# First layer, first sweep and the change to the second: the same operations issued at other slots

## The chip, the core and the metric

The kernel runs on one core of one Trainium2 chip. The metric is the device time of one execution in microseconds (us); each kernel is run several times and the median is compared. The core has TensorE (PE, with the load of its weights shown as PEld), VectorE (DVE), ScalarE (ACT), GpSimd (POOL) and SyncE (SP). Each engine takes its instructions in the order in which they are written for it, and waits at one until the semaphores it needs are there. POOL and SP do nothing here but start DMA transfers.

## The reference

Three steps follow one another. All arrays are fp32.

```
# attention: 8 batches x 8 heads, 576 positions in chunks of 64, head size 64
scores = (q_c @ k_c.T) / 8;  attn = softmax(scores);  out = attn @ v_c
x = out as (4608 tokens, 512)
# layer 1: w_gate, w_val 512 x 1536, w_out 1536 x 512
g = x @ w_gate;  x = (g * sigmoid(g) * (x @ w_val)) @ w_out
# layer 2: w_in 512 x 2048, w_out 2048 x 512
h = x @ w_in;  y = (h - tanh(h)) @ w_out
```

## The kernel before

**Numbers.** An fp32 operand is held as two fp32r tiles: a high half (a cast, step h...) and a low half (a subtraction of the high half from the operand, step l...). A product takes three passes (high by high, high by low, low by high). The high half is made by DVE or ACT, as the table ON says; the low half by DVE (`halves`, L436).

**Tiling.** The 4608 tokens are 9 batches of 512. A unit is one batch by one pair of 128 hidden columns. Sweep 0 does pairs 0 to 2 of layer 1 for all batches, sweep 1 pairs 3 to 5 (and adds the partial result x2p of sweep 0), sweep 2 the 8 pairs of layer 2. A name such as vs0_4_2_1 says sweep 0, batch 4, third unit, second column block. Each in-projection of a unit is made of seven products at 128x256 in place of eight (`product`, `in_proj`, L653 and L667). They run in the order B11, B21, T2, T1, T3, B22, T4, where T1 to T4 are sums of quarters of x and of w, into two PSUM banks X and Y (Xg, Yg for the gate, Xv, Yv for the values). Partial results are copied out on the way by ACT ("snaps": s<-Xv, s<-Yv), and DVE adds them to the bank later. The product that follows in the same bank waits for that copy or addition. A unit issues 14 products and 8 pieces of out-projection (acc), whose hidden tiles h are those of the unit two before it.

**Preparing x.** While a unit runs, x of the next batch is split for the seven products (`x_set`, L741): four sums (s0 to s3, subtractions on DVE), seven high halves (hB11 ...) and seven low halves (lB11 ...), in tiles xb14_B11 and so on. In sweep 0 x comes from attention. It is computed for four tiles of 128 rows a batch, during the units of the batch before: transposes of q and k on DVE (tq, tk: qT, kT, L873), scores on PE (sc, L887), maximum and difference on DVE for two halves (c0, c1: mx and scratch, L796 and L299), the exponential on ACT (e, L801), sum and reciprocal on DVE (n: sm, L805 to L807), the division on DVE (m, L302), a transposition on PE (ppt, L823), its copy by ACT, and the output on PE (po, L898), which ACT copies to xra (x of the next batch). Scores, ppt and po share the two PSUM banks a0 and a1.

**Order.** The tables at the head of the file set the order. AT gives each step a slot relative to the START of its set, ON the engine. One PE piece (a product, or a piece of out-projection, by the letters of PE) is written per slot, and then the steps that are due (`tick`, L311):

```
while later and later[0][0] < now[0] + 1:
    heapq.heappop(later)[-1]()
now[0] += 1
```

So a slot sets no time. It sets where a step stands in the queue of its engine, relative to the other steps of that engine. Between engines only semaphores order the work. Sets that matter here: a (attention tile), x0 (split of x in sweep 0), x1 (in sweep 1), g0 and g1 (silu, product and halves of h in sweep 0 and 1), ge (the same for the last units of sweep 0), fc1 and fr1 (weights for sweep 1: columns of w_gate and w_val, rows of w_out, read back from a scratch copy in HBM: f_wv, f_wo), ah (the preparation of that copy: magnitude on ACT, four bit operations on DVE; cvt_wv, raw_wv).

Of the kernel before, what the change touches and what calls it, by code (L numbers as in the profile page):

```python
# [29 lines left out]
    "ah.ld": -6.5, "ah.mag": 9.5, "ah.cl": 11.5, "ah.sh": 11.5, "ah.sg": 12.5, "ah.tl": 13,  # L30
# [12 lines left out]
    "g1.l0": 19.5, "g1.h1": 22, "g1.l1": 23, "a.lq": -19.5, "a.lv": 4, "a.tq": -8.5, "a.tk": -4,  # L43
    "a.s": 0, "a.c0": 1.5, "a.c1": 2.5, "a.e": 3, "a.n": 7, "a.m": 9, "a.p": 12.5, "a.o": 14.5,
    "ge.silu0": 14.5, "ge.silu1": 12.5, "ge.m1": 21, "ge.m0": 20.5, "ge.h0": 23, "ge.l0": 24.5,
    "ge.h1": 24, "ge.l1": 32, "dr.ld": -19.5, "dr.mag": 9, "dr.cl": 11, "dr.sh": 11.5,
    "dr.sg": 13, "dr.tl": 13, "dr.h": 16.5, "dr.l": 17.5, "dc.ld0": -14, "dc.mag0": 0,
# [1430 lines left out]
```

## Time and profile before

| | |
|---|---|
| median of 3 runs | 1757.7 us (1754.9 to 1758.71) |
| profiled execution | 1756.21 us, its span 1754.4 us |
| mean granted TensorE clock | 0.994 |
| PE busy | 1712.4 us, 98% of the span |
| DVE busy | 1381.9 us, 79% |
| ACT busy | 1135.8 us, 65% |
| POOL busy | 136.5 us, 8% |
| chain that ended last | PE 83%, DVE 8%, SP's queue 4%, DMA 3% |

The span runs from the first to the last instruction; the profiled execution's own time is 1.8 us longer. PE is busy almost all the time, so a change of order can only take or leave the short gaps in which PE waits for another engine. The reading therefore goes to PE's waits, then to what stood in the queue of the engine waited for.

### The profile page before, as it was taken

The page shows a single profiled execution, that of the slowest core. Times are in us where ns is not written, and L with a number is a line of the kernel's source. Part 1 is how long each engine was busy: PE and PEld are TensorE (multiplying, and loading weights), DVE is VectorE, ACT ScalarE, POOL GpSimd, SP SyncE. Part 2 cuts the span into 40 slices and gives each one's busy share as a digit, 9 for nine tenths or more (in the row PEclk, how much of TensorE's full clock was granted, in tenths as well). Part 3 has the DMA queues.
Part 4 walks back from the last instruction along what each step waited for, and adds up shares of the span by engine and source line. Part 5 has one row for each costly group of instructions (what it writes and reads, how often), then busy time and mean ns, then how long its engine had stood idle before and what let it go on. Part 6 is the DMA issues. An engine that isn't in the chain of part 4 may idle for free.

```text
span 1754.4 us, 33741 instructions
## 1 busy us (share of the span) xinstructions
PE 1712.4 (98%) x12880; PEld 1531.7 (87%) x12880; DVE 1381.9 (79%) x2613; ACT 1135.8 (65%) x2209; POOL 136.5 (8%) x238
## 2 busy tenths in 40 slices
PE   5999999999999999999999999999999999999999
PEld 4778888888898999999999898899999898998997
DVE  6998778887878987787875678787877878787876
ACT  4765565566555655545554578787777777777776
POOL 2133333322100000000000000000000000000000
PEclk8999999999999999999999999999999999999999
DMA  9554554555423555555545744343434343434333
GB/s 244 143 109 115 142 134 123 128 145 138 131 101 120 193 186 169 180 186 186 169 167 191 260 174 145 107 145 97 151 102 144 105 148 97 149 104 144 99 130 109
DMA packets 238482, 254.94 MB, mean 145 GB/s; under 512 B 150000, under 2 KB 175472, under 8 KB 236016
## 3 DMA queue, kind: packets, MB, share of 16 engines
q1 hardware_dynamic: 230896, 243.33, 45.4%
q0 software_dynamic: 7424, 9.45, 2.1%
q8 instruction: 101, 1.65, 0.4%
q14 instruction: 61, 0.50, 0.1%
HBM read 187.17 MB, written 65.54 MB: 144 GB/s over the span
## 4 chain that ended last, share of the span: by engine, by line
PE 83%; DVE 8%; SPq 4%; DMA 3%; ACT 1%; issue 1%; DVEq 0%; ACTq 0%
PE acc L1239 36%; PE Xi L660 12%; PE Yi L660 9%; PE Xg L660 6%; PE Xv L660 6%; PE Yv L660 5%; PE Yg L660 5%; SPq L849 3%; DMA raw_wv<-in_moe_w_val_dram 1%; SPq L947 1%; DMA kr<-in_k_dram 1%; DVE scratch L299 1%; PE po L898 1%; PE sc L887 1%; PE ppt L823 1%
## 5 line engine op out<-in xcount | busy, mean ns | idle before, releaser
L1239 PE MATMUL acc<-wp,h 128*128 128x512 f32 x1728 | 479.9, 394 | 0.0
L1239 PE MATMUL acc<-h,wo 128*128 128x512 f32 x1296 | 364.1, 397 | 0.0
L1239 PEld LDWEIGHTS acc<-wp,h 128*128 128x128 f32 x1728 | 290.9, 188 | 33.4 <-DVE h L299 0.3
L1239 PEld LDWEIGHTS acc<-h,wo 128*128 128x128 f32 x1296 | 220.4, 189 | 28.6
L338 ACT CAST h<-gs 128x512 fp32r<-128x512 f32 x144 | 89.5, 621 | 86.0 <-DVE gs L1150 84.5
L864 POOL DMA_DIRECT2D vr<-in_v_dram x200 | 116.2, 599 | 283.9 <-PE po L898 259.9
L660 PEld LDWEIGHTS Xg<-xb_T,wg 128*128 128x128 f32 x864 | 122.2, 188 | 13.0
L660 PE MATMUL Xg<-xb_T,wg 128*128 128x256 f32 x864 | 125.9, 281 | 0.0
L296 DVE TENSOR_TENSOR gs<-Yi,s 128x256 f32<-128x256 f32 x144 | 60.8, 422 | 64.9 <-PE Yi L660 59.5
L1073 ACT ACTIVATE gs<-gs 128x512 f32<-128x512 f32 x96 | 60.8, 633 | 58.0 <-DVE gs L296 57.8
L299 DVE TENSOR_TENSOR vr<-gs,vr 128x512 f32<-128x512 f32 x72 | 49.9, 692 | 54.6 <-ACT vr L1126 54.6
L299 DVE TENSOR_TENSOR h<-gs,h 128x512 fp32r<-128x512 f32 x144 | 92.7, 684 | 0.2 <-ACT h L338 0.2
L338 ACT CAST h<-vs 128x512 fp32r<-128x512 f32 x107 | 66.3, 622 | 37.1 <-PE acc L1239 25.2
L299 DVE TENSOR_TENSOR h<-vs,h 128x512 fp32r<-128x512 f32 x108 | 73.6, 682 | 20.3 <-ACT h L338 19.5
L660 PE MATMUL Yv<-xb_B,wv 128*128 128x256 f32 x576 | 85.4, 283 | 2.0 <-ACT s L338 1.9
L660 PE MATMUL Xv<-xb_T,wv 128*128 128x256 f32 x576 | 86.2, 285 | 0.8 <-ACT sqr L338 0.8
L660 PE MATMUL Yg<-xb_B,wg 128*128 128x256 f32 x576 | 84.2, 281 | 0.0
L660 PEld LDWEIGHTS Yg<-xb_B,wg 128*128 128x128 f32 x576 | 78.8, 189 | 5.1
L660 PEld LDWEIGHTS Yv<-xb_B,wv 128*128 128x128 f32 x576 | 75.4, 188 | 6.1 <-ACT s L338 4.6
L660 PEld LDWEIGHTS Xv<-xb_T,wv 128*128 128x128 f32 x576 | 75.1, 189 | 1.4 <-ACT sqr L338 1.0
L338 ACT COPY s<-Xi 128x256 f32<-128x256 f32 x144 | 53.5, 372 | 34.9 <-PE Xi L660 30.9
L302 DVE TENSOR_TENSOR vs<-vs,gs 128x512 f32<-128x512 f32 x96 | 65.8, 686 | 8.1 <-ACT gs L1073 5.3
(310 smaller groups left out, 3732.7 us busy)
## 6 DMA issues: line engine op xcount, KB each, us to landing
wp<-split_wp SPq DMA_DIRECT2D x144, 512.0 KB, 3.5
split_wi<-wi SPq DMA_DIRECT2D x24, 512.0 KB, 3.4
xd<-xra SPq DMA_DIRECT2D x36, 256.0 KB, 3.1
x2p<-ob SPq DMA_DIRECT2D x36, 256.0 KB, 2.6
xr_xd<-xd SPq DMA_DIRECT2D x9, 1024.0 KB, 4.8
ob<-x2p SPq DMA_DIRECT2D x36, 256.0 KB, 4.2
x2d<-ob SPq DMA_DIRECT2D x36, 256.0 KB, 2.4
xr_x2d<-x2d SPq DMA_DIRECT2D x9, 1024.0 KB, 6.0
```

The costliest lines, as they stand in the source:

```text
L296: eng.tensor_tensor(out=out_, in0=a, in1=b, op=ALU.add)
L299: eng.tensor_tensor(out=out_, in0=a, in1=b, op=ALU.subtract)
L302: eng.tensor_tensor(out=out_, in0=a, in1=b, op=ALU.mult)
L338: eng.copy(out_, in_)
L660: nc.tensor.matmul(bank, w[:, wl, kk * 128:(kk + 1) * 128], x[xn][:, xl, kk, :], start=start and n == 0, stop=n == 5, skip_group_check=not ...
L823: nc.tensor.transpose(pt[:, m, :], z["p"][:, m].rearrange("p e j -> p (e j)"), ident)
L849: nc.sync.dma_start(out=r[p:p + 32, 2 * n:2 * (n + m)], in_=src[b, 2 * j + e, s:s + m * C, d * 32:d * 32 + 32] .rearrange("(n p) d -> p n ...
L864: nc.gpsimd.dma_start(out=vr[p:p + C, n + skip:n + m:2], in_=chunks[:, skip:m:2],)
L887: nc.tensor.matmul(sc[e ^ c][c * C:(c + 1) * C, m, :], z["qT"][h, cut], z["kT"][h, cut], start=True, stop=True,)
L898: nc.tensor.matmul(po[c][h, m, :], z["vr"][f, 2 * m + c, :], z["pT"][f, m, c * C:(c + 1) * C], start=True, stop=True,)
L1073: return lambda: nc.scalar.activation(out=gs[i], in_=gs[i], func=AF.Silu)
L1239: nc.tensor.matmul(u["acc"][d], l, r, start=p0 and i == 0 and n == 0, stop=p1 and i == 1 and n == 2,)
```

## The change

Only numbers in the three tables change. No operation is added or removed. AT moves the steps of the sets ah, fc1, fr1, x0, g0, g1, a and ge; START moves the loads of the weights for sweep 1; ON changes six entries: five high halves of the x split of sweep 0 (hB11, hB21, hT2, hT3, hB22) go from DVE to ACT, the high half of the first w_out row (fr1.h0) from ACT to DVE. In total DVE has 33 instructions less, ACT 33 more.

```
-    "x0.s0": -9, "x0.hT1": 13.3, "x0.hT4": 15.3, "a.tq": -8.5, "a.n": 7, "a.p": 12.5, "a.o": 14.5,
+    "x0.s0": -13.5, "x0.hT1": 17.3, "x0.hT4": 20.3, "a.tq": -4.5, "a.n": 8, "a.p": 12, "a.o": 15,
...
-    "g1.silu0": 16, "g1.m1": 20.5, "g1.h0": 18.5, "g1.h1": 22, "g1.l1": 23,
+    "g1.silu0": 18, "g1.m1": 26, "g1.h0": 22, "g1.h1": 27.5, "g1.l1": 31.5,
...
-    "x0.hB11": 'V', "x0.hB21": 'V', "x0.hT2": 'V', "x0.hT3": 'V', "x0.hB22": 'V', "fr1.h0": 'A',
+    "x0.hB11": 'A', "x0.hB21": 'A', "x0.hT2": 'A', "x0.hT3": 'A', "x0.hB22": 'A', "fr1.h0": 'V',
```

These lines gather entries that stand apart in the file. What they do to the queues is seen in three places.

DVE in the third unit of batch 4, from the third sum of the x split to the division of attention tile 24 (scratch0 with sm24); xb14 is x of batch 5, vs0_4_2 the values of the running unit. Before:

```order
L299 TENSOR_TENSOR scratch1_2011<-xra5_3825,scratch1_2011 128x512
L296 TENSOR_TENSOR vs0_4_2_1_4559<-Xv0_4_2_4483,s0_4_2_4485 128x256
L299 TENSOR_TENSOR xb14_T2_4515<-scratch1_2011,xb14_T2_4515 128x512
L805 TENSOR_REDUCE sm24_4565<-scratch0_175 128x8
L806 TENSOR_SCALAR sm24_4565<-sm24_4565 128x8
L807 RECIPROCAL sm24_4565<-sm24_4565 128x8
L299 TENSOR_TENSOR xra5_3825<-scratch1_2011,xra5_3825 128x2x256
L873 STREAM_TRANSPOSE qT25_4570<-qr25_4401 128x512
L296 TENSOR_TENSOR vs0_4_2_0_4509<-Yv0_4_2_4484,s0_4_2_4485 128x256
L340 CAST xb14_T3_4580<-xra5_3825 128x512
L302 TENSOR_TENSOR scratch0_175<-scratch0_175,sm24_4565 128x512
```

and now:

```order
L299 TENSOR_TENSOR scratch1_2002<-xra5_3827,scratch1_2002 128x512
L299 TENSOR_TENSOR xb14_T2_4516<-scratch1_2002,xb14_T2_4516 128x512
L296 TENSOR_TENSOR vs0_4_2_1_4547<-Xv0_4_2_4485,s0_4_2_4487 128x256
L299 TENSOR_TENSOR xra5_3827<-scratch1_2002,xra5_3827 128x2x256
L296 TENSOR_TENSOR vs0_4_2_0_4510<-Yv0_4_2_4486,s0_4_2_4487 128x256
L805 TENSOR_REDUCE sm24_4571<-scratch0_175 128x8
L806 TENSOR_SCALAR sm24_4571<-sm24_4571 128x8
L807 RECIPROCAL sm24_4571<-sm24_4571 128x8
L302 TENSOR_TENSOR scratch0_175<-scratch0_175,sm24_4571 128x512
L299 TENSOR_TENSOR xb14_T1_4562<-xra5_3827,xb14_T1_4562 128x512
L299 TENSOR_TENSOR xb14_T3_4576<-xra5_3827,xb14_T3_4576 128x512
```

The casts to xb14 are gone from the queue, the low halves come earlier, and the transpose of q for tile 25 and the second vs0 addition no longer stand between the reciprocal and the division.

ACT at the same place, from the copy of Xg to the copy of the transposed probabilities of tile 24. Before:

```order
L338 COPY gs0_4_2_1_4391<-Xg0_4_2_4329 128x256
L338 COPY s0_4_2_4485<-Xv0_4_2_4483 128x256 x2
L801 ACTIVATE scratch0_175<-scratch0_175 128x512
L338 CAST xb14_T1_4525<-xra5_3825 128x512
L338 COPY s0_4_2_4485<-Yv0_4_2_4484 128x256
L1073 ACT_TABLE_LOAD
L1073 ACTIVATE gs0_4_2_0_4347<-gs0_4_2_0_4347 128x512
L338 CAST xb14_T4_4551<-scratch1_2011 128x512
L1073 ACTIVATE gs0_4_2_1_4391<-gs0_4_2_1_4391 128x512
L338 COPY vs0_4_2_1_4559<-Xv0_4_2_4483 128x256
L338 COPY scratch0_175<-ppt24_4607 128x512
```

and now, from the first casts on:

```order
L338 CAST xb14_B11_4500<-xra5_3827 128x512
L338 CAST xb14_B21_4502<-xra5_3827 128x512
L338 CAST xb14_T2_4516<-scratch1_2002 128x512
L338 COPY s0_4_2_4487<-Xv0_4_2_4485 128x256
L801 ACTIVATE scratch0_175<-scratch0_175 128x512
L338 COPY s0_4_2_4487<-Yv0_4_2_4486 128x256
L1073 ACT_TABLE_LOAD
L1073 ACTIVATE gs0_4_2_0_4347<-gs0_4_2_0_4347 128x512
L338 CAST xb14_T1_4562<-xra5_3827 128x512
L1073 ACTIVATE gs0_4_2_1_4391<-gs0_4_2_1_4391 128x512
L338 CAST xb14_T3_4576<-xra5_3827 128x512
L338 COPY vs0_4_2_1_4547<-Xv0_4_2_4485 128x256
```

Three casts stand ahead of the second copy of Xv and of the exponential (L801), T1 and T3 behind it; T4 and B22 follow.

ACT at the change of sweep, in the last unit of sweep 0 and the first of sweep 1 (wo3 and wv4 are weights for sweep 1, xb26 is x of batch 0 for sweep 1, cvt_wi0 belongs to layer 2). Before:

```order
L338 CAST xb26_T4_7493<-xr_xd0_89_7006 128x512
L338 CAST wo3_1_7505<-f_wo3_7357 128x512
L338 CAST wg4_3_7333<-f_wv4_7373 128x256
L338 CAST wv4_0_7513<-f_wv4_7373 128x2x256
L338 COPY vs0_8_2_1_7501<-Xv0_8_2_7439 128x256
L367 ACTIVATE cvt_wi0_7540<-raw_wi0_7416 128x512
L338 CAST wv4_2_7549<-f_wv4_7373 128x2x256
L338 COPY s1_0_0_7557<-Xg1_0_0_7555 128x256
L338 CAST wv4_1_7570<-f_wv4_7373 128x2x256
L338 COPY sqr1_0_0_7575<-Xv1_0_0_7573 128x256
```

and now:

```order
L338 CAST xb26_T3_7514<-xr_xd0_89_7007 128x512
L338 COPY vs0_8_2_1_7497<-Xv0_8_2_7441 128x256
L1073 ACTIVATE gs0_8_2_1_7409<-gs0_8_2_1_7409 128x512
L367 ACTIVATE cvt_wi0_7530<-raw_wi0_7412 128x512
L338 CAST xb26_T4_7532<-xr_xd0_89_7007 128x512
L338 CAST xb26_B22_7541<-xr_xd0_89_7007 128x512
L338 CAST wo3_1_7545<-f_wo3_7414 128x512
L338 CAST wv4_0_7547<-f_wv4_7375 128x2x256
L338 COPY s1_0_0_7552<-Xg1_0_0_7550 128x256
L338 COPY sqr1_0_0_7568<-Xv1_0_0_7566 128x256
L338 CAST h0_8_2_0_7585<-vs0_8_2_0_7465 128x512
L338 CAST wv4_2_7595<-f_wv4_7375 128x2x256
```

The cast of wo3_1 now stands behind the split of x and the copy to vs0_8_2_1, that of wo3_0 is no longer on ACT, and the copy sqr1_0_0 stands ahead of the casts of h and wv4_2. On SP the load of f_wo3 now stands behind those of f_wv4 and raw_wi0; before it stood ahead of both.

On PE one thing moves: the output po is written one piece later, so that only one piece stands between po and the next tile's scores.

## Rows read from the trace of the kernel before

**Rows 1.** Waits of PE, 160 to 600 us: total, times, longest.
```profile
PE ppt L823 <- DVE scratch L302: 5.4, 5, 1.1
PE Yv L660 <- ACT s L338: 1.9, 6, 0.6
PE Yg L660 <- DVE gs L296: 1.7, 1, 1.7
PE Xg L660 <- DVE vs L296: 1.1, 1, 1.1
...
PE Xv L660 <- ACT sqr L338: 0.8, 1, 0.8
```

**Rows 2.** Windows: batch 4's third unit, the next, one of sweep 1; length, PE, PEld, DVE, ACT, POOL.
```profile
313.40:334.60 21.20, 19.62 (x185) 16.89 (x183) 18.62 (x41) 11.28 (x23) 4.69 (x8) 1.00 0.59 142
334.60:353.70 19.10, 18.95 (x240) 16.74 (x239) 14.54 (x32) 11.22 (x22) 7.11 (x13) 1.00 0.38 96
...
603.50:619.10 15.60, 15.60 (x110) 14.54 (x109) 12.63 (x26) 8.08 (x19) 0.00 (x0) 1.00 0.34 119
```

**Rows 3.** Timeline of PE, third unit of batch 4: start, busy, operation, idle before.
```profile
320.60 0.69 PE L898 MATMUL po<-scratch,vr 64*64 64x64 f32 x32 [0.22 <-ACT scratch L338]
...
327.18 0.88 PE L660 MATMUL Xv<-xb_T,wv 128*128 128x256 f32 x6
327.89 0.86 PE L1239 MATMUL acc<-h,wo 128*128 128x512 f32 x3
329.00 0.97 PE L660 MATMUL Yv<-xb_B,wv 128*128 128x256 f32 x6 [0.24 <-ACT s L338]
330.02 0.98 PE L660 MATMUL Xv<-xb_T,wg 128*128 128x256 f32 x6
330.85 2.26 PE L1239 MATMUL acc<-h,wo 128*128 128x512 f32 x9
334.17 0.63 PE L823 MATMUL ppt<-ident,scratch 128*128 128x128 f32 x4 [1.07 <-DVE scratch L302]
```

**Rows 4.** Timeline of DVE in the same unit.
```profile
327.42 0.42 DVE L340 CAST xb_T<-scratch 128x512 fp32r<-128x512 f32 x1
327.75 1.29 DVE L299 TENSOR_TENSOR xb_B<-xra,xb_B 128x512 fp32r<-128x512 f32 x2
...
332.08 0.70 DVE L873 STREAM_TRANSPOSE qT<-qr 128x512 f32<-128x512 f32 x1
332.71 0.39 DVE L296 TENSOR_TENSOR vs<-Yv,s 128x256 f32<-128x256 f32 x1
...
333.34 0.68 DVE L302 TENSOR_TENSOR scratch<-scratch,sm 128x512 f32<-128x512 f32 x1
```

**Rows 5.** Timeline of ACT in the same unit.
```profile
325.96 0.38 ACT L338 COPY s<-Xv 128x256 f32<-128x256 f32 x1 [1.07 <-PE Xv L660]
327.53 0.64 ACT L801 ACTIVATE scratch<-scratch 128x512 f32<-128x512 f32 x1 [1.20 <-DVE scratch L299]
328.07 0.60 ACT L338 CAST xb_T<-xra 128x512 fp32r<-128x512 f32 x1
328.58 0.37 ACT L338 COPY s<-Yv 128x256 f32<-128x256 f32 x1
...
334.83 0.59 ACT L338 COPY scratch<-ppt 128x512 f32<-128x512 f32 x1 [2.38 <-PE ppt L823]
```

**Rows 6.** Timeline of ACT at the change of sweep.
```profile
551.21 0.62 ACT L338 CAST wo<-f_wo 128x512 fp32r<-128x512 f32 x1
...
558.01 0.62 ACT L338 CAST wv<-f_wv 128x512 fp32r<-128x512 f32 x1 [1.65 <-DVE f_wv L299]
```

**Rows 7.** Timeline of DVE at the change of sweep.
```profile
551.87 0.69 DVE L299 TENSOR_TENSOR wo<-f_wo,wo 128x512 fp32r<-128x512 f32 x1 [0.88 <-ACT wo L338]
...
561.85 0.41 DVE L296 TENSOR_TENSOR gs<-Yg,s 128x256 f32<-128x256 f32 x1
```

**Rows 8.** DMA issues 536 to 540 us: count, KB, us from issue to landing.
```profile
raw_wi<-in_moe_w_in_dram SPq DMA_DIRECT2D x1, 512.0 KB, 6.7
```

More of the change, by code (lines that the diff above doesn't have):

```diff
@@ L29 @@
 AT = {
-    "ah.ld": -6.5, "ah.mag": 9.5, "ah.cl": 11.5, "ah.sh": 11.5, "ah.sg": 12.5, "ah.tl": 13,
[12 rows of a table removed]
[L43 to L47, printed above, removed]
[100 rows of a table removed]
+    "ah.ld": -14, "ah.mag": 6.5, "ah.cl": 12, "ah.sh": 12.5, "ah.sg": 13.5, "ah.tl": 14,
[13 rows of a table added]
+    "a.tq": -4.5, "a.tk": -4, "a.s": 0, "a.c0": 1.5, "a.c1": 2.5, "a.e": 3, "a.n": 8, "a.m": 9,
+    "a.p": 12, "a.o": 15, "ge.silu0": 7.5, "ge.silu1": 19, "ge.m1": 21.5, "ge.m0": 20,
+    "ge.h0": 24.5, "ge.l0": 25.5, "ge.h1": 26.5, "ge.l1": 32, "dr.ld": -19.5, "dr.mag": 9,
+    "dr.cl": 11, "dr.sh": 11.5, "dr.sg": 13, "dr.tl": 13, "dr.h": 16.5, "dr.l": 17.5,
[100 rows of a table added]
 }
```

237 rows, old and new, of tables (AT, ON, START) are left out of this document.

## The prediction, made before the changed kernel ran

> **Bounds.** I read the share of busy time first, then the waits of TensorE (PE) by line, then windows of single units, then the timelines of PE, VectorE (DVE) and ScalarE (ACT) through one unit and through the change of sweep. PE is busy 98% of the span, so only its few idle gaps can be won: an order moves no work off PE. In the stretch that holds batches 2 to 8 of sweep 0 and the change to sweep 1, nearly all of PE's idle time has five causes [rows 1]. The reader is to see that two of them repeat: five waits for the softmax division, 5.4 us in all, and six for a copied half product, of which the longest is 0.6. They recur in the third units of batches 2 to 6. The other three causes are single waits at the change of sweep. In one such third unit PE is idle 1.58 us (21.20 less 19.62), while a unit of sweep 1 has PE busy for all of its 15.60 us [rows 2]: later stretches have little to give, and something to lose.
>
> **The loss.** In a third unit, six products take 0.71 us from start to start (327.18 to 327.89) and three out-projection matmuls 0.70 (busy 0.86 against 0.88). So after 327.89 the next product was due at 328.59, the one after at 329.30 and the out-projection at 330.01; it started at 330.85, 0.84 late. Its nine matmuls need 2.10, so the transposition of the probabilities was due at 332.95 and came at 334.17: 1.22 late. The attention output at 320.60 waited 0.22 [rows 3]. Together 2.28 us. The idle time alone gives 1.58 as the lower bound; I take 2.25, which is what passes on PE's clock, times five units: 11.2 us.
>
> **Why late.** DVE works in order. Ahead of the division at 333.34 stand casts of 0.33 (327.42 to 327.75), a transpose of q for the next tile of 0.63 (332.08 to 332.71), and the low half of a hidden tile [rows 4]. The change gives five of DVE's seven casts of the x split to ACT, puts the q transpose of the next tile and the low half of h behind the division. Ahead of the division that takes away four casts (1.32), the transpose (0.63) and one 128x512 subtraction (0.60, by the first of the pair at 327.75, 1.29 for two): 2.55 us. The division then could start at 330.8 and end at 331.4, or later where it meets new waits; the transposition would be due at 334.17 less 2.28, at 331.9. The margin is 0.5 at best, and I count on 0.2, since the second sum of the division's tile now follows directly on an addition that waits for PE. So the 1.22 goes.
>
> The late product at 329.00 waited for ACT's copy of Yv at 328.58, which stood behind the exponential at 327.53 and a cast; the exponential in turn waited 1.20 for DVE's second centring [rows 5]. Two casts and the low half (1.27 us) leave DVE ahead of that centring, so the exponential can start near 326.3 and the copy, due once its product ends (327.18 plus 0.16), is done before 328.0, ahead of the 328.59 at which it is wanted. The addition on Xv that held the product of 330.02 also comes earlier by the casts that stood ahead of it (1.0). So the 0.84 goes as well. The 0.22 goes because the copy of the transposed probabilities now runs ahead of a cast on ACT, and the output is issued one piece later.
>
> What ACT takes on: three casts between its copies of Xv and the exponential, two more behind them. A cast of this size takes ACT 0.51 from start to start (328.07 to 328.58). Three are 1.5 us; ACT waited 1.07 ahead of the copy at 325.96, 1.20 ahead of the exponential and 2.38 ahead of the copy at 334.83 [rows 5]. So the casts lie in idle time, with 0.1 to 0.3 us of delay for the copy that follows the third; that copy is not the one PE waits for. If that cover were gone, each cast would cost PE 0.51.
>
> The Trainium skill, page "VectorE: DVE Perf Modes", section on the TRN2 errata, speaks against this swap: its formulas give a copy of 512 fp32 elements about 0.33 us on VectorE and 0.61 on ScalarE, an estimate from that page. The trace agrees on the direction, with 0.42 busy for the cast on DVE [rows 4] and 0.60 on ACT [rows 5]. By that rule the 33 casts that change engine would take the two engines some 9 us more, and if all of it fell on PE's path the gain would be 6 and not 15; whether PE sees any of it is the first rival.
>
> **Costs.** With the output one piece later, only one piece stands between it and the next tile's scores, which use the same two banks and need both copies of the output. I cannot see that wait in the trace, since it did not occur. From below nothing; from above the length of ACT's nearest copy out of PSUM, 0.59 [rows 5], at some 20 tiles 12 us. The copies end about when the one piece does, so I take 0.07 a tile: 1.3 us. For the middle units, where a division and a copy now stand behind other work, I take 0.3 in all, between nothing and one more wait as long as the old one of the output (0.22) in five batches, 1.1.
>
> **First units** of the batches: the one of batch 5 has 0.15 us of idle time in 19.10 [rows 2], with the restart some 0.25 to 0.3, at one addition that stood behind a q transpose (0.63, as above), now moved behind it. I take 1.2 for five; the bounds are 0 and 1.5.
>
> **The change of sweep.** PE lost 0.6 (in the copy row), 1.1, 0.8 and 1.7 us of idle time, 4.2 in all [rows 1]; with the restarts and two small gaps that I read from its starts it is 5.3. Their causes stand in the engines' rows: ACT's second cast of wo came at 551.21, so DVE sat 0.88 idle at 551.87 and its addition came late; the copy of Xv stood behind ACT's cast of wv at 558.01, which had waited 1.65 for DVE; the addition on Yg came at 561.85, behind DVE's backlog [rows 6, 7]. In the changed order the wo cast stands behind the x split and the first copy, the copy of Xv ahead of the h and wv casts, and the casts are off DVE (1.7 us of backlog). The first two waits go, the third shrinks to 0.3 or so: I take 4.0 of 5.3; the bounds are 0 (each replaced) and 5.3. The wo weights now are fetched third, behind the others; the transfer that was third took 6.7 us to land [rows 8], and with the issue read from SP's queue (about 537.4) wo would land at 544.1; the first wo cast, now on DVE, stands at about 544.3. The margin is 0.2 only.
>
> The loads of q and k are issued up to two pieces later on SP and those of v on POOL two or three; the order on these queues still gives each tile's transfer more than one tile's time before its transpose or output, so I cost them at nothing; a transfer that came late would show as a DVE transpose waiting, up to the 6.7 of [rows 8].
>
> The start of sweep 2 gains 0.25 by one low half moved. Sweep 1 and 2 themselves: nothing, hidden by an engine that is 19% idle there (DVE 12.63 of 15.60) [rows 2].
>
> **The sum.** 11.2 + 1.2 + 4.0 + 0.25 less 1.3 and 0.3 = 15.05 us. The profiled execution took 1756.2 with a span of 1754.4, so it would be 1741.2; it lay 1.5 us under the median of 1757.7, so the median comes to 1742.6; I forecast 1743.
>
> **Rivals.**
> 1. ACT becomes the late engine: a T2 cast that waits for DVE's sum, ahead of the copies and the exponential, or a cast between output and scores. For it: three casts in a row ahead of a copy that PE waits for. Against: ACT's idle stretches of 1.07 and 2.38. Half of the third units' gain is left, 5.6, and the scores cost 3 rather than 1.3: 15.05 − 5.6 − 1.7 = 7.7 faster, 1750. Chance 0.15.
> 2. The change of sweep wins nothing, because wo lands late and DVE, in order, stands still behind its cast. For it: the margin of 0.2. Then 15.05 − 4.0 = 11, 1747. Chance 0.13.
> 3. Slower: in sweep 1 the gate steps were moved (silu, products and casts of h two to eight pieces later). If a copy or an addition there comes after PE wants it, every one of its 27 units stalls. A wait as long as the scratch copy's (0.22) costs 6 us and leaves 9 of the gain; from 0.56 us a unit (15.05 over 27) the kernel is slower, and at 0.75, the Xv wait of [rows 1], it is 20 − 15 = 5 slower, 1763. Against: PE never waits there now, DVE has 3 us free in 15.6 and the hidden tile is used only two units on. Chance 0.06.
> 4. No change: the division is late for another reason (the exponential, not DVE's queue), each wait is followed by the next one, and only 2 or 3 us remain: 1755 to 1758. Chance 0.08.
> The forecast, with 12 to 18 us won, has 0.58.
>
> **Numbers.** A measurement of this kernel can tell about 0.2%, 3.5 us, from no change. Faster by more: the forecast, rivals 1 and 2, 0.86; within: 0.08; slower: 0.06. The best case has all losses gone and no new cost (11.4 + 1.5 + 5.3 + 0.3 = 18.5, 1739); a little is left out below 1737. Up to 1753 the range holds rivals 1 and 2; rivals 3 and 4 lie above it.
>
> **What shows it.** In the waits of PE the row of the division falls from 5 waits to at most one, the copy row from 6 to at most two, the three single rows fall under 0.5 us each. The third units take about 19.0 us instead of 21.2. DVE's busy time falls by about 14 us (33 casts at 0.42), ACT's rises by about 20 (33 at 0.62). A new row on PE for the scores waiting for ACT's output copy would be the 1.3 us; if it is over 3 us, the first rival holds. A wait of DVE for the fetched wo near 544 shows the second. Units of sweep 1 longer than 15.6 show the third. The forecast is wrong if the division's row keeps over 2 us.

## The result and the profile after

The changed kernel takes 1739.0 us (median of 4 runs, 1738.1 to 1740.6), the kernel before 1758.2 in the runs beside it; the ratio is 0.9895, with a 95% interval of 0.9877 to 0.9912. By the ratio that is 18.5 us or 1.05% faster (by the medians 19.2); 1743 was forecast, and 1739 was its best case. The span of the profiled execution fell from 1754.4 to 1737.0 us, by 17.4. The casts that change engine are 32 and not 33: 35 leave DVE, three come to it (the page of the profile counts 2613 instructions on DVE before, 2581 after).

The waits of PE between 160 and 600 us, where the five causes of [rows 1] came to 10.9 us (and two smaller ones to 1.1), have one row left (total, times, longest):

```profile
PE Yg L660 <- ACT s L338: 0.5, 1, 0.5
```

The windows that answer to [rows 2], the third unit of batch 4, the unit behind it and one of sweep 1 (length, PE, PEld, DVE, ACT, POOL):

```profile
307.80:326.70 18.90, 18.90 (x185) 17.04 (x183) 16.94 (x36) 13.73 (x28) 4.51 (x8) 1.00 0.64 157
326.70:345.40 18.70, 18.70 (x240) 16.83 (x238) 14.71 (x31) 11.22 (x23) 6.31 (x11) 1.00 0.39 93
...
585.80:601.40 15.60, 15.60 (x109) 14.54 (x108) 13.18 (x27) 7.64 (x19) 0.00 (x0) 1.00 0.33 119
```

The reader is to see that the profile shows PE busy for all of each window, that five casts have left DVE (41 instructions became 36) and come to ACT (23 became 28), and that a unit of sweep 1 still takes 15.60. The same places on PE as in [rows 3]:

```profile
320.61 0.88 PE L660 MATMUL Yv<-xb_T,wv 128*128 128x256 f32 x6
321.33 0.88 PE L660 MATMUL Xv<-xb_T,wv 128*128 128x256 f32 x6
322.04 0.87 PE L1239 MATMUL acc<-h,wo 128*128 128x512 f32 x3
322.75 0.87 PE L660 MATMUL Yv<-xb_B,wv 128*128 128x256 f32 x6
323.45 0.94 PE L660 MATMUL Xv<-xb_T,wg 128*128 128x256 f32 x6
324.23 2.26 PE L1239 MATMUL acc<-h,wo 128*128 128x512 f32 x9
326.33 0.60 PE L823 MATMUL ppt<-ident,scratch 128*128 128x128 f32 x4
```

From the out-projection at 322.04 to the transposition it is now 4.29 us; in [rows 3] it was 6.28 (327.89 to 334.17). DVE there, answering to [rows 4]:

```profile
314.91 0.67 DVE L299 TENSOR_TENSOR h<-vs,h 128x512 fp32r<-128x512 f32 x1
...
322.94 0.42 DVE L296 TENSOR_TENSOR vs<-Xv,s 128x256 f32<-128x256 f32 x1
...
323.87 0.42 DVE L296 TENSOR_TENSOR vs<-Yv,s 128x256 f32<-128x256 f32 x1
324.20 0.68 DVE L805 TENSOR_REDUCE sm<-scratch 128x8 f32<-128x512 f32 x1
...
325.36 0.69 DVE L302 TENSOR_TENSOR scratch<-scratch,sm 128x512 f32<-128x512 f32 x1
```

The row at 314.91 is the low half of h. The division ends at 326.05, and the transposition starts at 326.33: 0.28 us, where the prediction counted on 0.2. The addition on Xv ends at 323.36, and the product behind it starts at 323.45: 0.09 us. ACT, answering to [rows 5]:

```profile
320.11 0.62 ACT L338 CAST xb_T<-scratch 128x512 fp32r<-128x512 f32 x1
320.63 0.36 ACT L338 COPY s<-Xv 128x256 f32<-128x256 f32 x1
320.90 0.63 ACT L801 ACTIVATE scratch<-scratch 128x512 f32<-128x512 f32 x1
321.53 0.37 ACT L338 COPY s<-Yv 128x256 f32<-128x256 f32 x1
```

The copy of Yv ends at 321.90, 0.85 us before its product at 322.75; the copy of Xv ends at 320.99, 0.34 us before its product at 321.33.

The gain by stretch, from the start of one unit's first product to the next one's: the third units of batches 2 to 6 took 105.97 us together and now take 94.23 (21.19 and 18.85 each); the first units of batches 2 to 7 114.58 and 112.55; the middle ones 105.78 and 106.62; the three units of batch 8 with the first two of sweep 1, the change of sweep, 83.48 and 78.66. Together 17.75. What is left is some tenths: the first unit of sweep 2 is 0.18 shorter, its third 0.30 longer, the start of the program 0.11 and its end 0.30 longer. These differ between runs whatever the change; the time to the first unit of batch 2 goes from 159.3 to 161.6 us over the 14 profiles.

### The profile page after: what moved, and what is told of

Its sections match the earlier page's. It is cut to its first block, busy times and chain, and to the rows that moved or that the text cites. A ratio compares the mean times of both kernels' runs of the same rounds, so it can differ in the third digit from the quotient of the medians.

```text
span 1737.0 us, 33830 instructions
## 1 busy us (share of the span) xinstructions
PE 1707.1 (98%) x12880; PEld 1533.8 (88%) x12880; DVE 1374.1 (79%) x2581; ACT 1143.3 (66%) x2241; POOL 135.8 (8%) x238
## 4 chain that ended last, share of the span: by engine, by line
PE 92%; DVE 3%; SPq 1%; DMA 1%; ACT 1%; issue 0%; DVEq 0%; ACTq 0%
PE acc L1239 39%; PE Xi L660 12%; PE Yi L660 9%; PE Xv L660 8%; PE Xg L660 8%; PE Yg L660 6%; PE Yv L660 6%; PE po L898 1%; SPq L947 1%; PE sc L887 1%; PE ppt L823 1%; PE Xg L715 1%; PE Yv L715 1%; DMA raw_wv<-in_moe_w_val_dram 0%; SPq L849 0%
## 5 line engine op out<-in xcount | busy, mean ns | idle before, releaser
L296 DVE TENSOR_TENSOR gs<-Yg,s 128x256 f32<-128x256 f32 x96 | 40.0, 417 | 55.7 <-PE Yg L660 32.6
L660 PEld LDWEIGHTS Yg<-xb_B,wg 128*128 128x128 f32 x576 | 78.6, 189 | 6.1 <-ACT s L338 1.0
L338 ACT COPY gs<-Xg 128x256 f32<-128x256 f32 x48 | 17.9, 372 | 97.4 <-PE Xg L660 96.5
```

Of the source, the lines that this page charges most:

```text
L296: eng.tensor_tensor(out=out_, in0=a, in1=b, op=ALU.add)
L338: eng.copy(out_, in_)
L660: nc.tensor.matmul(bank, w[:, wl, kk * 128:(kk + 1) * 128], x[xn][:, xl, kk, :], start=start and n == 0, stop=n == 5, skip_group_check=not ...
```

## The experiments

Twelve kernels ran. Times are medians; the third, first and sweep columns are unit times read from PE's starts as above, the third ones of batches 2 to 6 and the first ones of batches 3 to 6, as means.

| kernel | us | third unit | first unit | change of sweep |
|---|---|---|---|---|
| before | 1758.2 | 21.19 | 19.13 | 83.5 |
| changed | 1739.0 | 18.85 | 18.76 | 78.7 |
| casts_only | 1749.9 | 20.03 | 19.13 | 83.9 |
| attn_only | 1751.8 | 20.29 | 19.07 | 84.5 |
| other_only | 1755.5 | 20.43 | 19.58 | 81.8 |
| split_attn_only | 1746.5 | 19.43 | 18.75 | 83.0 |
| casts_back | 1747.8 | 19.71 (median) | 19.08 | 80.6 |
| attn_back | 1746.0 | 19.26 | 19.57 | 79.1 |
| g0_back | 1743.3 | 19.44 | 18.75 | 79.7 |
| fr1_back | 1741.4 | 18.82 | 18.75 | 80.3 |
| act_plus1 | 1743.1 | 19.26 | 18.75 | 78.8 |
| act_plus3 | 1749.5 | 20.42 | 18.75 | 80.3 |
| wo_first | 1740.1 | 18.82 | 18.75 | 78.6 |
| better2 | 1739.2 | 18.82 | 18.75 | 79.1 |

The kernel before had medians of 1756.6 to 1757.0 beside the twelve and 1758.2 beside the changed kernel. So a difference to the changed kernel, below, is good to some 2 us (five of the twelve also have two executions only), and the argument goes by the units.

The theory behind the forecast: in a third unit DVE's order decides, and casts, transpose and low half of h add up ahead of the division. The rivals: only the places of transpose and low half count; or ACT, with three casts more ahead of its copies, is late in turn.

**casts_only**

```
-    "x0.hB11": 'V', "x0.hB21": 'V', "x0.hT2": 'V', "x0.hT3": 'V', "x0.hB22": 'V',
+    "x0.hB11": 'A', "x0.hB21": 'A', "x0.hT2": 'A', "x0.hT3": 'A', "x0.hB22": 'A',
```

> The kernel before, with nothing but the five high halves of the x split moved from DVE to ACT; every slot as before. Theory A (the length of DVE's queue ahead of the division decides): four casts, 1.3 us, are gone ahead of the division, so the five waits of PE for it fall from 1.1 to 0.2 or less each and a third unit takes 19.6 to 20.0 us instead of 21.2; in all 6 to 9 us faster. Theory B (it is where the q transpose and the low half of h stand): the waits stay above 0.7 each and the whole gains under 3 us. Theory C (ACT becomes late): the copy row of PE grows above 3 us and the whole is no faster.

It is 6.7 us faster than before (ratio 0.9962, 0.9947 to 0.9977). The third units are at the edge of what theory A gave, but not by its way. PE's waits, 160 to 600 us (in this kernel and the next ones line numbers can be 2 or 4 higher), then the division and the transposition in batch 4:

```profile
PE ppt L825 <- DVE scratch L304: 3.5, 5, 0.7
...
PE po L900 <- ACT scratch L340: 0.9, 4, 0.2
PE Yv L662 <- ACT s L340: 0.4, 1, 0.4
```

```profile
330.47 0.67 DVE L304 TENSOR_TENSOR scratch<-scratch,sm 128x512 f32<-128x512 f32 x1
```

```profile
331.29 0.63 PE L825 MATMUL ppt<-ident,scratch 128*128 128x128 f32 x4 [0.71 <-DVE scratch L304]
```

What went are the waits for the copy of Yv in the third units. This unit starts at 311.60, so the division starts 18.87 us into it, where it was 19.98 before: 1.1 earlier. PE starts the out-projection ahead of the transposition 0.76 earlier, so its wait falls only from 1.1 to 0.7. The bound of 0.2 was wrong.

**attn_only**: the kernel before with the new a.* slots.

```
-    "a.tq": -8.5, "a.n": 7, "a.p": 12.5, "a.o": 14.5, "a.lq": -19.5, "a.lv": 4,
+    "a.tq": -4.5, "a.n": 8, "a.p": 12, "a.o": 15, "a.lq": -18, "a.lv": 6.5,
```

> The kernel before with the new slots of the attention steps alone (a.*: q transpose, sum, transposition, output, loads). Theory A: only the transpose (0.63) goes from ahead of the division, and the wait for the output (0.22 to 0.38 with its restart): third units 20.2 to 20.5, 4 to 5 us faster in all; the first units lose their 0.3. Theory B: the five waits for the division fall below 0.3, third units under 19.7, 8 us or more faster.

4.8 us faster (0.9973, 0.9962 to 0.9984), third units 20.29: theory A's numbers, the total in part by luck (in the profiled execution the change of sweep lost 1.1 and the start of the program won 1.1). The wait for the division is halved by the one transpose that left, and the wait for the output is gone:

```profile
PE ppt L825 <- DVE scratch L304: 2.4, 5, 0.5
PE Yv L662 <- ACT s L340: 1.9, 6, 0.6
```

The first units gained only 0.06, since here the scores of one tile came 0.34 us late: their second part starts at 334.31, 0.05 after ACT's second copy of the output ends, and the copies had started only at 333.61, right behind the end of DVE's last low half of x (333.54). The cost that the prediction feared exists in this order, and not in the changed one, where the copies end 0.09 us ahead of the scores.

**other_only**: the kernel before with the changes to ah, fc1, fr1 (its first cast on DVE too), g0, g1, ge and START alone.

> The kernel before with all that is not attention and not the x split of sweep 0: weights for sweep 1, gate steps, preparation of weights, START. Theory A: batches 2 to 7 of sweep 0 as before (third units 21.2, within 0.2), the change of sweep 4 to 5 us faster, sweep 1 still at 15.60 a unit: 4 to 5 us faster in all. Rival: the change of sweep needs the freed DVE of the last x split as well (three or four casts in that unit), then under 2.5 us faster.

```profile
PE ppt L827 <- DVE scratch L306: 5.4, 5, 1.1
PE Yv L664 <- DVE vs L300: 4.5, 8, 1.0
PE Yg L664 <- DVE gs L300: 1.1, 1, 1.1
```

Not to be told from before (0.9993, 0.9984 to 1.0003). Theory A was wrong twice. The third units fell by 0.76 (the waits for the output and for the copy of Yv are gone), so the slots of the gate or of the weights' preparation do act in the batches; the first units rose by 0.45 at an addition that stands behind a transpose of q. And the change of sweep gained 1.7, not 4 to 5: the rival holds, it needs the x split as well.

**split_attn_only**: x0 and a as in the changed kernel, the rest as before.

> The kernel before with the new slots and engines of the x split (x0) and the new slots of attention (a), nothing else of the change. Theory A (in a third unit DVE's order decides, and casts, transpose and low half add up): 18.9 to 19.3 us a third unit, no wait for the division above 0.3, 9 to 11 us faster from the batches. The change of sweep: the casts off DVE there help too, 1 to 2 us. In all 10 to 13 us faster. Rival (the parts hide one another, as they are paid once): the three parts taken alone gave 1.1, 0.9 and 0.75 us a third unit, and two of them together give at most 1.6: third units above 19.6.

10.5 us faster (0.9942, 0.9926 to 0.9959), as theory A said in total, but the third units are 19.43, between both expectations, and the change of sweep gained 0.5 only. The wait for the division is gone altogether, and PE waits elsewhere:

```profile
PE Xv L660 <- DVE vs L296: 2.0, 5, 0.4
PE Xv L660 <- ACT sqr L338: 1.5, 1, 1.5
PE Xg L660 <- DVE vs L296: 1.1, 1, 1.1
```

The first row is five third units: the addition on Xv, behind the low half of h.

**g0_back**: the changed kernel with the old gate slots of sweep 0.

```
-    "g0.silu0": 15.5, "g0.h0": 24.5, "g0.h1": 29, "g0.l1": 31,
+    "g0.silu0": 15, "g0.h0": 23, "g0.h1": 27, "g0.l1": 34.5,
```

> The changed kernel with the four old slots of the gate set of sweep 0 (silu0, h0, h1, l1). The low half of the last hidden tile then stands between the reciprocal and an addition in the first units, and its cast on ACT ahead of the copy of the transposed probabilities. Theory A: first units 0.2 to 0.7 us longer each, third units within 0.2 (the output is written a piece later, which covers the copy): 1.5 to 4 us slower. Rival (the slots of the gate do not matter): within 1 us.

```profile
PE Xv L660 <- DVE vs L296: 2.4, 6, 0.4
```

```profile
321.86 0.68 DVE L299 TENSOR_TENSOR h<-vs,h 128x512 fp32r<-128x512 f32 x1
...
325.66 0.42 DVE L296 TENSOR_TENSOR vs<-Xv,s 128x256 f32<-128x256 f32 x1
```

4.2 us slower than the changed kernel, a little more than expected and at other places: 0.6 in each third unit (0.56 lost at the addition on Xv), 1.05 at the change of sweep, nothing in the first. In this unit, which starts at 309.96, the low half of h stands between two additions on DVE, and the addition on Xv starts 15.70 us into the unit; in the changed kernel the low half stands ahead of the scores' maximum (314.91, shown above) and the addition starts at 15.11. So l1, 31 instead of 34.5, moves the low half of h (0.60 on DVE), and by that frees the addition on Xv. It and split_attn_only show the same wait from both sides.

**casts_back**: the changed kernel with the five casts back on DVE.

> The changed kernel with the five high halves back on DVE, all new slots kept. Theory A: the division is late again by four casts (1.3 us) less the margin of some 0.3 to 0.5, so PE waits 0.8 to 1.0 at each of five divisions and for one copy each; 6 to 9 us slower than the changed kernel, third units near 20.3. Theory B: under 2 us slower, third units under 19.2.

```profile
PE Xv L662 <- DVE vs L298: 3.1, 5, 0.8
PE Yv L662 <- DVE vs L298: 2.8, 3, 1.9
```

8.7 us slower than the changed kernel, theory A's total, but not its parts. The third units take 19.7 and not 20.3, 0.8 to 0.9 more, and PE waits at the additions, not once in these units at the division; the change of sweep takes 2.0 more, and the first units 0.3, where the scores come 0.34 late as in attn_only. One third unit, of batch 3, took 22.39, 2.7 more than the others of its run. There a transpose of k came 2.2 us late on DVE; the transfers that bring k:

```profile
262.61 0.71 DVE L875 STREAM_TRANSPOSE kT<-kr 128x512 f32<-128x512 f32 x1 [2.24 <-issue]
```

```profile
L851 SPq DMA_DIRECT2D kr<-in_k_dram x8: 385/458/752, 255.0 to 258.9; - x8
...
DMA to landing us min/median/max: 1.9/2.4/3.5
```

The last of the eight was issued at 258.9 and took the longest, 3.5, so it landed at 262.4, 0.2 us ahead of the transpose. By these times DVE waited for the late load, as the prediction said that such a load would show, and these 2.7 are not DVE's queue. The profiled execution is the longest of the four (1749.1; the others 1746.5 to 1748.3). In the changed kernel the same transfer landed 0.8 us ahead of its transpose (257.8, 258.6). Why it took longer here is open.

**attn_back**: the changed kernel with the old a.* slots.

> The changed kernel with the old slots of the attention steps. Theory A: the q transpose (0.63) is ahead of the division again; the margin of 0.2 to 0.5 goes, third units 19.0 to 19.5 with a wait for the division of 0.1 to 0.5 each; the first units get back the late addition, 0.2 to 0.3 each. 2 to 5 us slower than the changed kernel. Rival (margin over 0.7): within 1 us of it.

7.0 us slower, where 2 to 5 were expected: third units 0.3 to 0.7 longer (mostly 0.30 ahead of the transposition), as expected; first units 0.8 longer, more than expected, at an addition behind the transpose of q:

```profile
PE Yv L660 <- DVE vs L296: 3.6, 7, 0.6
```

**fr1_back**: the changed kernel with the old slots of w_out's rows, and their first cast back on ACT.

```
-    "fr1.ld": -2.5, "fr1.h0": 2, "fr1.l0": 8.5, "fr1.h1": 12.5, "fr1.l1": 15,
+    "fr1.ld": -10, "fr1.h0": 6.5, "fr1.l0": 9, "fr1.h1": 9, "fr1.l1": 10.5,
...
-    "fr1.h0": 'V',
+    "fr1.h0": 'A',
...
-    "fo10": -13, "fo11": 50.5,
+    "fo10": -15, "fo11": 54,
```

> The changed kernel with the rows of w_out for sweep 1 (fr1) at their old slots, loaded first again, their first cast back on ACT. Theory: the cast of wo waits on ACT for its buffer, ahead of copies, and PE stalls again at one product by 0.6 to 1.5 us in the last unit of sweep 0; 0.5 to 2.5 us slower in all, all of it in the units around the change of sweep. Rival: x split and gate slots won the 4.8 us there alone: within 0.4 us in those units.

1.6 us longer at the change of sweep, 1.25 of it in the last unit of sweep 0, as expected. ACT's timeline there, then PE's wait:

```profile
536.22 0.62 ACT L338 CAST wo<-f_wo 128x512 fp32r<-128x512 f32 x1 [3.16 <-PE acc L1239]
```

```profile
PE Xg L660 <- DVE vs L296: 1.1, 1, 1.1
```

The second cast of wo holds ACT for 3.16 us until an out-projection has freed its buffer, DVE's low half of wo waits for that cast, and the addition behind it keeps PE waiting, as in [rows 6, 7]. The wait that was 1.1 before is this one.

**act_plus1** and **act_plus3**: the changed kernel with one or all three of the casts ahead of the exponential done twice (lines of the function of the halves).

```
-            copy(eng, z["t"][0], src())
+            for _ in range(2 if (step.name, x) in [('x0', 'T2')] else 1): copy(eng, z["t"][0], src())
```

> The changed kernel with one of the three casts ahead of the exponential (T2) done twice on ACT, 0.52 us more ACT work in each third unit, the same values written. Theory (the casts lie in ACT's idle time: the copy of Yv ends 0.85 us before PE wants it): third units within 0.1 us of 18.85, the whole within 1 us of the changed kernel. Rival (ACT is at its edge): 0.5 us a third unit, 2.5 us or more in all.

> The changed kernel with all three casts ahead of the exponential (B11, B21, T2) done twice, 1.56 us more ACT work there. Theory: the cover of 0.85 us is used up; the copy of Yv ends 0.6 to 0.8 late, third units 19.4 to 20.0 and a wait of PE for that copy in five or six units, 3 to 6 us in all. Rival (ACT has more room than read, or DVE decides anyway): within 0.2 us a unit.

One cast more costs 0.41 a third unit, three cost 1.57. The rival of the first holds (0.5 was its number). PE and ACT in batch 4 with one more:

```profile
321.37 0.87 PE L660 MATMUL Yv<-xb_T,wv 128*128 128x256 f32 x6
322.48 0.98 PE L660 MATMUL Xv<-xb_T,wv 128*128 128x256 f32 x6 [0.24 <-ACT s L338]
```

```profile
320.88 1.27 ACT L338 CAST xb_T<-scratch 128x512 fp32r<-128x512 f32 x2
322.06 0.36 ACT L338 COPY s<-Xv 128x256 f32<-128x256 f32 x1
```

PE waits for the copy of Xv, the first behind the casts, and not for that of Yv. With three more the row of PE's waits, and the same two places in batch 4, are:

```profile
PE Xv L660 <- ACT s L338: 9.8, 7, 1.4
```

```profile
323.89 0.87 PE L660 MATMUL Yv<-xb_T,wv 128*128 128x256 f32 x6
326.17 0.98 PE L660 MATMUL Xv<-xb_T,wv 128*128 128x256 f32 x6 [1.41 <-ACT s L338]
```

```profile
325.75 0.36 ACT L338 COPY s<-Xv 128x256 f32<-128x256 f32 x1
```

Counted from the start of the product into Yv, the copy of Xv ends after 0.38 us in the changed kernel, 1.05 with one more cast and 2.22 with three; the product into Xv starts after 0.72, 1.11 and 2.28. So the copy moves by 0.67 and 1.84, the product by 0.39 and 1.56: ACT's room there is 0.28 us, and all beyond it lands on PE.

**wo_first**: the rows of w_out loaded first again, all else as changed.

```
-    "fr1.ld": -2.5,
+    "fr1.ld": -8,
```

> The changed kernel with the rows of w_out for sweep 1 loaded ahead of the columns again, everything else as changed. Theory (DVE's wait of 1.83 us for that load is hidden): the wait goes, the units around the change of sweep stay within 0.1 us each, the whole within 1 us. Rival (the wait pushes DVE late and causes what is left there): the unit that has 0.98 us of stalls falls under 16.2 us.

The change of sweep is the same within 0.1 us. In the changed kernel DVE stood still until the load was there, and here it does not:

```profile
531.19 0.43 DVE L340 CAST wo<-f_wo 128x512 fp32r<-128x512 f32 x1 [1.83 <-DMA f_wo<-f_wo]
```

```profile
530.12 0.42 DVE L340 CAST wo<-f_wo 128x512 fp32r<-128x512 f32 x1
```

So the wait is hidden, by 0.34 us: in the changed kernel the addition behind it in DVE's queue ends at 532.56, and the product that needs it starts at 532.90.

**better2**: the changed kernel with three numbers more, each against one of the waits that were left.

```
+    "y1.lT1": 25.2, "fc1.s2": 10, "dc.h0": 11.5,
```

> The changed kernel with three numbers more: the low half of T1 of the first x split of sweep 2 ahead of a low half of h (y1.lT1 25.2), a difference of weights behind an addition (fc1.s2 10), a cast of layer 2 weights behind the copy of Yg (dc.h0 11.5). Theory: the three waits that PE still has at the two changes of sweep (0.29, 0.69 and 0.92 us) go, 1.5 to 1.9 us faster than the changed kernel in the span. Rival: each is followed by the next wait, under 0.5 us; or a cast moved in every unit pair of sweep 1 costs there, slower.

Its 1739.2 cannot be told from 1739.0 (its ratio to before is 0.9903, 0.9887 to 0.992). By units the first number does what it should: the first unit of sweep 2 goes from 11.60 to 10.58 and its wait is gone. The two others win 0.24 in the first unit of sweep 1 and lose 0.51 in the next; the last unit of sweep 0 is 0.16 longer. PE's waits in that stretch:

```profile
PE Xg L660 <- ACT s L338: 0.2, 1, 0.2
PE Yv L660 <- DVE vs L296: 0.2, 1, 0.2
```

The first number by itself, worth 1.0 by this count, was not run.

## Why the prediction was right, and where not

The main mechanism held. PE's waits in the third units came from work queued ahead on DVE, and nearly all of it went: 11.7 us measured where the sum had 11.2. The division starts 2.45 us earlier in its unit (17.53 instead of 19.98); 2.55 was the prediction's figure.

**Which move took which wait** was read wrongly in three steps. The prediction put the low half of h behind the division; it went ahead of the scores' maximum, by g0.l1, and in the changed order what it frees is the addition on Xv (g0_back, 0.56). The wait for the output was put down to the order on ACT and to the later output together; attn_only and other_only each took it away alone, so one of the two was enough. And the casts were counted for both the copy and the division; casts_only shows that they took the copy's wait, while the division's stayed at 0.7, because PE arrives earlier by what it has just won. Taken alone the three groups win 1.16, 0.90 and 0.76 us a third unit, 2.82 in all; together, and with the slots of the x split, which were in none of the three, 2.34: parts of a wait were paid for twice. What those slots do by themselves was not run.

**ACT's cover** is the step that was wrong in kind. The prediction said that the copy behind the third cast is not the one PE waits for. It is the next that PE waits for: one cast more and PE loses 0.41. The rows of idle time [rows 5] are real, but the idle time ahead of an instruction that waits for PE is no room for work unless PE can wait too. That the casts cost PE nothing here is luck, by 0.28 us; one cast more would have cost some 2.5 of the 17.4 (0.41 in five third units, 0.48 in that of batch 7). In casts_only the five casts alone leave ACT 17.5 us busier and DVE 10.6 less: they are dearer on ACT, and PE gained all the same.

**The scores behind the output** were given 1.3 us; they cost nothing measurable in the changed order, and 0.34 us in the first units of attn_only and of casts_back. This is the largest term that was mis-sized.

**First units**: 1.2 forecast, 2.0 measured, over its upper bound of 1.5: 0.37 in each of five batches and 0.16 in the sixth, where it had 0.25 to 0.3 in five. The addition's wait is all of it: in the unit of batch 5 the out-projection ahead of that product took 1.01 us to the next start (346.24 to 347.25), now 0.71 (338.42 to 339.12), and the product itself lost 0.10 more. **Middle units**: 0.3 forecast, 0.84 measured, 0.14 in each of six. No wait shows there, but PE's starts place it. In all six the sixth product of the gate, into Yg, took 0.71 us to the next start and now takes 0.80 (to 295.83 in batch 4). There, PE and then ACT:

```profile
295.03 0.96 PE L660 MATMUL Yg<-xb_B,wg 128*128 128x256 f32 x6
```

```profile
294.02 0.68 ACT L367 ACTIVATE cvt_wv<-raw_wv 128x512 f32<-128x512 f32 x1
294.60 0.36 ACT L338 COPY s<-Yg 128x256 f32<-128x256 f32 x1
```

The copy that this product needs ended 0.64 us ahead of it before; now it stands behind the magnitude of the weights (ah.mag, 9.5 to 6.5) and ends 0.07 ahead. other_only has the same margin and the same 0.80; casts_only and attn_only have neither. The other 0.06 is that of attn_only, at the output, which stands one piece later.

**The change of sweep**: 4.0 forecast, 4.8 measured. The causes were right for the wo cast (fr1_back). The margin of 0.2 for the load was wrong: the load took 6.8 us as third (524.31 to 531.10), against 6.7 in [rows 8], but DVE came to the cast 1.83 before it. So what the second rival feared, DVE standing still, did happen, and cost PE nothing, by 0.34 us (wo_first). What the prediction did not see is that neither part wins it alone: x split and attention 0.5, everything else 1.7, both 4.8; with all but the five casts it is 2.9 (casts_back).

**Sweep 1** stayed at 15.60 in all but its first unit, so the rival with a new wait per unit did not occur. The page's busy times fell by 7.8 us on DVE and rose by 7.5 on ACT, where 14 and 20 were forecast from single durations. Instructions that overlap their neighbours are counted once there: in casts_only 35 casts make 10.6 and 17.5, or 0.30 and 0.50 each. The rest is the new order elsewhere: from the third unit of sweep 1 to its last, with the same work, DVE is 3.1 us busier and ACT 6.4 less (12.63 and 8.08 a unit in [rows 2], now 13.18 and 7.64).

The errors leave a sum of 15.05 against 17.4 in the span: 0.5 more from the third units, 0.8 from the first, 0.8 from the change of sweep and 1.3 not paid, less 0.5 in the middle units and 0.6 at the start, in sweep 2 and at the end.

## What to carry to other kernels

Before adding work to an engine's idle time, find which instruction ends that idle time and who waits for its result: room is the distance from the end of that result to the moment it is wanted, not the length of the gap. When several things queue ahead of one late instruction, taking away one moves the consumer too, so gains of single moves do not add; undo each part in the finished kernel as well as trying it alone. A wait that disappears leaves the next-latest instruction as the bound, here within 0.1 us.

## What was not expected of the hardware

After the waits read here PE loses more than the idle time shown. In act_plus1 the product at 322.48 starts 0.39 us late with 0.24 shown, and takes 0.81 to the next start where 0.71 is usual: 0.49 in all. The first 0.15 is in the counting: a row's busy time of 0.87 runs 0.15 past the next start, 0.72 after its own, and idle time is counted from its end. The 0.10 is time that passes on PE, and it shows without a late start too: two products whose releaser ended 0.07 and 0.09 us ahead of them took 0.80 and 0.78 (295.03 and 323.45 above). A sum of idle times therefore understates such waits by some 0.25 each, and leaves out those that end just in time.

The third of three transfers of 512 KB issued within a microsecond landed 6.7 us after its issue in the kernel before and 6.8 in the changed one, where it carries another tile (7.0 in fr1_back, 6.9 in wo_first). So its landing could be reckoned with to 0.3 us; when DVE would come to it could not.
